# One joint routing job for the first batch's keys and first queries, a second job for its other queries, and query blocks of varying width

## The chip, the cores and the metric

The kernel runs on one core of one Trainium2 chip. The metric is the device time of one execution in microseconds (us), lower is better. Executions carry a state, fast or slow, and only fast ones enter the ratios. All profiles shown are of executions in the fast state.

Engines are named as in the profile: PE is TensorE, PEld its weight loads, DVE is VectorE, ACT is ScalarE, POOL is GpSimd, SP is SyncE. Names such as L102 are lines of the kernel in question, so they differ between kernels.

## The reference

Attention in which a query sees only the keys with the same nearest centroid, then an expert layer over all tokens:

```python
batch, n_heads, seq, head_dim, n_clusters = 4, 8, 768, 64, 16
q_assign = argmax(q_n @ c_n)            # nearest of 16 centroids, for each head
k_assign = argmax(k_n @ c_n)
mask     = q_assign[:, :, :, None] == k_assign[:, :, None, :]
scores   = where(mask, q @ k.T / sqrt(64), -1e9)
x        = softmax(scores) @ v          # then heads side by side: 3072 tokens x 512
h        = x @ w_in                     # 512 -> 2048
out      = (h * sigmoid(h)) @ w_out     # 2048 -> 512
```

## The kernel before

Heads are handled in pairs; a batch has four pairs, and the first batch is the one that nothing can hide. For each pair the fp32 queries and keys are loaded (`nat`), split into a high and a low fp16 half (`hl`), transposed (`abt`; by PE in the first batch, by a transposing DMA later), multiplied with the split centroids (`psL`), and routed. Routing is a list of VectorE instructions: transpose the products (`lt`), take the maximum over each 16 (`mx`), compare (`oht`), transpose back (`ohu`). The resulting one-hot rows are copied below the queries and keys, so that one matmul (`st`) gives score plus mask. Then come the exponential (`P`, ACT), the product with the values (`pv`, PE), the division (`xh`, VectorE), a transposition (`xt`), and the expert layer: `ph` with `win_s`, tanh (`tn`, ACT), the gate (`gt`, VectorE), `po` with `wout_s`, and the store.

The first batch is routed pair by pair, and a block is always 256 queries wide:

```python
def load(p, t):                                      # one load per pair, queries or keys
    nat = mp.tile([128, 2, NJ * D], f32, name=f"nat{t}", bufs=3)
    nc.sync.dma_start(nat, (q, k)[t][b, 2 * r : 2 * r + 2]. ...)

def split_hi(p, t, eng):
    hl = hls[p, t] = mp.tile([128, 2 * NJ, 2, D], f16, name="hl", bufs=5)
    ...
groups = {}
for pl in [[p] for p in range(HB)] + [[p, p + 1] for p in range(HB, NP, 2)]:   # first batch: single pairs
    groups[pl[-1]] = pl
```

The centroids are split into halves on POOL, ahead of POOL's own loads (values `vt`, then the weights `win_s` and `wout_s`):

```python
def centroid_split():
    cn = mp.tile([128, D], f32, name="cn")
    nc.gpsimd.tensor_scalar(out=cn, in0=craw, scalar1=cw, scalar2=OHV, op0=ALU.mult, op1=ALU.mult)
    for n in range(2):
        nc.gpsimd.tensor_copy(ch2[:, n, :], cn)
    for n in range(2):
        nc.gpsimd.tensor_tensor(out=cl2[:, n, :], in0=cn, in1=ch2[:, n, :], op=ALU.subtract)
```

One property of the program matters for all that follows. A list scheduler inside the kernel simulates the engines while the kernel is being built, and writes each engine's instructions in the order that its own estimates give. On the chip this order is fixed: an engine whose next instruction waits does nothing, even if a later one could run (the changed kernel's VectorE stands 7.43 us in this way, see below).

The softmax here doesn't subtract the row's maximum and nothing guards it: scores larger than these inputs give would overflow.

## Time and profile before

| | before |
|---|---|
| time, median of 3 | 322.22 us (321.57 to 322.32) |
| span of the profiled execution | 322.0 us |
| first routing (VectorE `lt`) | 14.56 us |
| first exponential (ACT `P`) | 19.64 us |
| first expert matmul (PE `ph`) | 47.68 us |
| useful PE work of the whole program | 290 us |
| PE time lost by 60 us | 28.9 us |

"PE time lost by X" is X less the useful PE work begun by X, each matmul counted at the duration that it has where matmuls stand back to back (for 128 columns, which only the changed kernels have in `st` and `ph`, 56 ns, see below). It is read from the trace, and it is the yardstick for everything below, because between 60 us and the tail this kernel loses nothing. In all kernels below the account falls by 2 to 4 us between 60 and 300 us unless said otherwise, because those unit durations are slightly high.

The lines that carry the reading of the bound are in the prediction. One more view is needed, because the result turned on it. These are POOL's first instructions in the timeline of the kernel before (columns: start us, busy us, engine, line, operation, out<-in, shape, count, and in brackets the idle time before and what ended it):

```profile
5.16 0.31 POOL L346 TENSOR_SCALAR cn<-craw,cw 128x64 f32<-128x64 f32 x1 [3.54 <-DVE cw L342]
...
7.88 6.95 POOL L89 DMA_DIRECT2D vt<-in_v_dram  x8
```

POOL waits 3.54 us for the centroids' norm, splits them, and only then, at 7.88 us, issues the value loads. The reader should see that this small job is also a lock on the value loads, which nobody wrote down as one.

### The profile page before, as it was taken

The page shows a single profiled execution, that of the slowest core. Times are in us where ns is not written, and L with a number is a line of the kernel's source. Part 1 is how long each engine was busy: PE and PEld are TensorE (multiplying, and loading weights), DVE is VectorE, ACT ScalarE, POOL GpSimd, SP SyncE. Part 2 cuts the span into 40 slices and gives each one's busy share as a digit, 9 for nine tenths or more (in the row PEclk, how much of TensorE's full clock was granted, in tenths as well). Part 3 has the DMA queues.
Part 4 walks back from the last instruction along what each step waited for, and adds up shares of the span by engine and source line. Part 5 has one row for each costly group of instructions (what it writes and reads, how often), then busy time and mean ns, then how long its engine had stood idle before and what let it go on. Part 6 is the DMA issues. An engine that isn't in the chain of part 4 may idle for free.

```text
span 322.0 us, 7812 instructions
## 1 busy us (share of the span) xinstructions
PE 302.5 (94%) x3316; PEld 225.5 (70%) x3316; DVE 190.2 (59%) x356; ACT 239.3 (74%) x279; POOL 35.3 (11%) x57
## 2 busy tenths in 40 slices
PE   6688795999999999999989999999999999999994
PEld 4565574876877768777677777777777787786651
DVE  5798983675856878438328877338444344254431
ACT  5896994985678979886878787886787787786420
POOL 4952100024000000023200000040000000000000
PEclk9799998999999999999999999999999999999999
DMA  7999999999926990394996970293310200200001
GB/s 213 289 240 239 235 186 149 214 149 132 223 67 183 210 231 9 77 129 61 191 243 155 223 147 11 75 166 25 69 41 17 66 35 28 74 0 35 33 35 65
DMA packets 89843, 40.00 MB, mean 124 GB/s; under 512 B 75216, under 2 KB 86224, under 8 KB 89808
## 3 DMA queue, kind: packets, MB, share of 16 engines
q1 hardware_dynamic: 62032, 32.16, 44.1%
q0 software_dynamic: 27776, 7.34, 22.8%
q8 instruction: 26, 0.43, 0.6%
q14 instruction: 9, 0.07, 0.1%
HBM read 27.30 MB, written 6.29 MB: 104 GB/s over the span
## 4 chain that ended last, share of the span: by engine, by line
PE 78%; DMA 9%; DVE 9%; ACT 1%; issue 1%; SPq 1%; DVEq 0%
PE ph L276 25%; PE po L298 24%; PE st L213 16%; PE pv L229 9%; DMA abt<-hl 6%; PE psL L155 3%; DMA nat<-in_q_dram 2%; DMA xt<-xh 2%; DVE hl L102 1%; DVE abt L205 1%; DVE ohu L187 1%; DVE lt L162 1%; DVE hl L97 1%; DVE mx L173 1%; DVE oht L180 1%
## 5 line engine op out<-in xcount | busy, mean ns | idle before, releaser
L219 ACT ACTIVATE P<-st,bias 128x1024 f16<-128x1024 f32 x144 | 156.7, 1114 | 36.6 <-PE st L213 36.1
L285 DVE SCALAR_TENSOR_TENSOR gt<-tn,ph 128x512 f16<-128x512 f32 x96 | 65.1, 683 | 61.1 <-ACT tn L282 60.4
L276 PE MATMUL ph<-xt,win_s 128*128 128x256 f16 x768 | 97.1, 274 | 4.1 <-DVE xh L243 3.3
L298 PE MATMUL po<-wout_s,gt 128*128 128x512 f16 x384 | 96.5, 379 | 1.1 <-DVE ot L307 1.1
L213 PE MATMUL st<-abt 80*128 80x256 f16 x576 | 85.5, 274 | 4.0 <-ACT abt L203 1.6
L276 PEld LDWEIGHTS <-win_s 128*128 128x128 f16 x768 | 74.1, 98 | 18.1 <-DVE xh L243 3.6
L282 ACT ACTIVATE tn<-ph,zbias 128x512 f32<-128x512 f32 x96 | 65.3, 686 | 25.3 <-PE ph L276 24.7
L213 PEld LDWEIGHTS <-abt 80*128 80x128 f16 x576 | 55.1, 98 | 26.5 <-issue 3.7
L298 PEld LDWEIGHTS <-gt 128*128 128x128 f16 x384 | 35.9, 97 | 29.1 <-issue 1.6
L89 POOL DMA_DIRECT2D vt<-in_v_dram x32 | 26.5, 833 | 174.0 <-PE pv L229 165.2
L229 PE MATMUL pv<-vt,P 128*128 128x65 f16 x1152 | 43.3, 193 | 0.2 <-ACT P L219 0.2
L229 PEld LDWEIGHTS <-P 128*128 128x128 f16 x1152 | 41.8, 98 | 2.1 <-ACT P L219 0.3
L102 DVE SCALAR_TENSOR_TENSOR hl<-nat,hl 128x768 f16<-128x768 f32 x32 | 29.8, 956 | 2.8 <-ACT hl L95 2.5
L307 DVE TENSOR_SCALAR ot<-po 128x512 f32<-128x512 f32 x24 | 16.5, 686 | 24.2 <-PE po L298 24.1
L242 DVE RECIPROCAL rz<-pv 128x4 f32<-128x4 f32 x48 | 8.6, 178 | 28.0 <-PE pv L229 27.6
L243 DVE TENSOR_TENSOR xh<-pv,rz 128x256 f16<-128x256 f32 x48 | 20.4, 424 | 1.7
L97 DVE TENSOR_SCALAR hl<-nat 128x768 f16<-128x768 f32 x19 | 10.4, 556 | 5.3 <-DMA abt<-hl 5.2
L268 PE MATMUL warm<-idle,ident 128*128 128x256 f16 x66 | 11.7, 316 | 1.7 <-POOL ident masks.py:199 1.7
L95 ACT ACTIVATE hl<-nat 128x768 f16<-128x768 f32 x13 | 11.0, 843 | 2.6 <-DMA nat<-in_q_dram 2.2
L155 PE MATMUL psL<-abt,wh 128*32 128x512 f16 (+1 forms) x128 | 10.5, 340 | 0.7 <-DVE abt L122 0.4
L187 DVE STREAM_TRANSPOSE ohu<-oht 128x768 f16<-128x768 f16 x10 | 9.8, 977 | 0.9 <-DVE oht L180 0.5
L117 PE MATMUL ptt<-ident,hl 128*128 128x128 f16 x96 | 7.7, 235 | 2.7 <-ACT abt L122 1.9
(52 smaller groups left out, 100.4 us busy)
## 6 DMA issues: line engine op xcount, KB each, us to landing
nat<-in_q_dram SPq DMA_DIRECT2D x16, 384.0 KB, 5.2
nat<-in_k_dram SPq DMA_DIRECT2D x16, 384.0 KB, 5.6
out_dram<-ot SPq DMA_DIRECT2D x24, 256.0 KB, 2.1
vt<-in_v_dram POOLq DMA_DIRECT2D x32, 96.0 KB, 5.1
win_s<-in_moe_w_in_dram POOLq DMA_DIRECT2D x4, 512.0 KB, 13.2
wout_s<-in_moe_w_out_dram POOLq DMA_DIRECT2D x4, 512.0 KB, 22.9
abt<-oh SPq DMA_DIRECT2D x48, 24.0 KB, 2.0
abt<-hl SPq DMA_TRANSPOSE x24, 4.5
```

The source lines that it names most:

```text
L89: nc.gpsimd.dma_start(vts[p % NV][:, h, :, 0:D], v[b, 2 * r + h].rearrange("(p j) d -> p j d", j=NJ))
L102: nc.vector.scalar_tensor_tensor(out=hl[:, :, 1, :], in0=nat, scalar=128.0, in1=hl[:, :, 0, :], op0=ALU.mult, op1=ALU.subtract)
L155: nc.tensor.matmul(psL[g : g + 32, 0 : hi - lo], w, x[:, lo:hi], start=first, stop=last)
L213: nc.tensor.matmul(st[:, a, h, :], ab[0:K, 1, h, ts(2 * s + a, 128)], ab[0:K, 0, h, ts(u, UQ)], start=True, stop=True)
L219: nc.scalar.activation(out=P, in_=sts.pop((n, s)), func=AF.Exp, bias=bias32, scale=ESC)
L229: nc.tensor.matmul(out[:, e, h, :], P[:, a, h, ts(e, 128)], vts[p % NV][:, h, 2 * s + a, 0 : D + 1], start=(s + a + h + e == 0), stop=(s = ...
L243: nc.vector.tensor_tensor(out=xhs[c][:, :, r], in0=out[:, :, :, 0:D], in1=rz.unsqueeze(3).to_broadcast([128, 2, 2, D]), op=ALU.mult)
L276: nc.tensor.matmul(ph[:, e].rearrange("p (g x) -> p g x", g=2), win_s[:, r, ts(2 * f + e, 128)], xts[c][:, :, r, :], start=(r == 0), stop= ...
L282: nc.scalar.activation(out=tn, in_=phs[c, f], func=AF.Tanh, bias=zbias, scale=0.5)
L285: nc.vector.scalar_tensor_tensor(out=gts[c][:, 2 * f : 2 * f + 2, :], in0=tns.pop((c, f)), scalar=1.0, in1=phs.pop((c, f)), op0=ALU.add, o ...
L298: nc.tensor.matmul(pos[c, s], gts[c][:, fc, ts(s, 128)], wout_s[:, fc, :], start=(fc == 0), stop=(fc == NFB - 1))
L307: eng.tensor_scalar(out=ot, in0=pos.pop((c, s)), scalar1=0.5, scalar2=None, op0=ALU.mult)
```

## The change

The intent is to start the expert layer earlier. The keys of all four pairs and their first 256 queries (1024 columns) are routed in one job instead of four; the other 512 queries follow in a second job. The first batch's query blocks are 128, 128, 256 and 256 wide, so the first expert block needs less attention work ahead of it. For this the query loads are cut into a part "A" (first 256 queries) and a wide part "B" (the other 512). Besides, the centroid split moves from POOL to ACT and VectorE, there are eight split buffers instead of five, nine for exponentials instead of twelve, and the scheduler gets new estimates, a `HOLD` for POOL's loads and a table of hand-made rank shifts (`PLAN`).

```diff
+    SPAN = {"K": (0, NJ), "A": (0, 2), "B": (2, NJ)}
...
-    def load(p, t):
+    def load(p, t, v, eng):
-        nat = mp.tile([128, 2, NJ * D], f32, name=f"nat{t}", bufs=3)
+        nat = mp.tile([128, 2 * NJ * D], f32, name=f"nat{t}", bufs=4)[:, 0 : 2 * (hi - lo) * D]
...
+        hl = hls[p, t, v] = mp.tile([128, 2 * NJ, 2, D], f16, name="hl", bufs=8)[:, 0:n]
...
+    def logits0(v):
+        if v == "K":
+            both = ps.tile([128, 2, 512], f32, name="psL2", tag="st", bufs=2)
+            outs = [(both[:, 0], 1, 0, 512), (both[:, 1, 0:256], 1, 512, 768), (both[:, 1, 256:512], 0, 0, 256)]
+        else:
+            psL = ps.tile([128, 512], f32, name="psL", tag="moe", bufs=3)
+            outs, tl = [(psL, 0, 256, 768)], [psL]
...
-    def centroid_split():
-        cn = mp.tile([128, D], f32, name="cn")
-        nc.gpsimd.tensor_scalar(out=cn, in0=craw, scalar1=cw, scalar2=OHV, op0=ALU.mult, op1=ALU.mult)
+    def centroid_high():
         for n in range(2):
-            nc.gpsimd.tensor_copy(ch2[:, n, :], cn)
+            nc.scalar.mul(ch2[:, n, :], craw, cw)
+    def centroid_low():
         for n in range(2):
-            nc.gpsimd.tensor_tensor(out=cl2[:, n, :], in0=cn, in1=ch2[:, n, :], op=ALU.subtract)
+            nc.vector.scalar_tensor_tensor(out=cl2[:, n, :], in0=craw, scalar=cw, in1=ch2[:, n, :], ...)
...
+    HOLD = 7.8
+    W0 = (1, 1, 2, 2)
+    RK = {'K': -395, 'A': -400, 'B': -270}
...
+    def held(t):
+        return t > HOLD - 1e-6
...
+            {"POOL": 1.8}, lambda e: load_v(p), ..., when=from_slot(begins[p] - LEAD_V) if b else held, dma=(1.25, 2.0, 1.0),
+            wins = [Piece({"POOL": 0.6}, lambda e, r=r: e.dma_start(win_s[:, r], win_v[:, r]), (), rank=-6, when=held, ...)]
...
+    PLAN = {12: (40, 0), 15: (-4, 0), ...}
```

The cuts are marked with dots; the functions that use these names change accordingly.

## The prediction

> **What bounds the kernel now.** I read the page first (busy shares, the 40 slices), then the stretches, then the chain of waits, then the timeline of the first 60 us. The page:
>
> ```profile
> PE 302.5 (94%) x3316; PEld 225.5 (70%) x3316; DVE 190.2 (59%) x356; ACT 239.3 (74%) x279; POOL 35.3 (11%) x57
> ...
> PE   6688795999999999999989999999999999999994
> ```
>
> PE is full from the eighth slice on. So what can still be won lies in the first 60 us and in the tail. The stretches say the same (columns: length, then busy us and count of PE, PEld, DVE, ACT, POOL; clock, DMA share, GB/s):
>
> ```profile
> 10.00:15.00 5.00, 3.90 (x47) 2.80 (x47) 4.92 (x8) 4.47 (x10) 4.83 (x6) 0.76 1.68 271
> 15.00:20.00 5.00, 3.85 (x38) 3.11 (x36) 4.77 (x10) 4.38 (x7) 3.50 (x6) 0.89 1.85 236
> 20.00:25.00 5.00, 4.85 (x69) 3.63 (x69) 4.88 (x9) 5.00 (x7) 1.65 (x3) 1.00 1.08 232
> ...
> 80.00:120.00 40.00, 40.00 (x440) 29.78 (x438) 28.77 (x49) 31.11 (x38) 1.07 (x2) 1.00 0.90 181
> ```
>
> From 10 to 25 us VectorE (third pair) is busy 14.6 of 15 us: it bounds the start. PE's own digits there flatter it, for they hold warming matmuls and modelled ends. So I priced PE's useful work from pieces of the chain that stand back to back: 8 ph 0.872 us, 4 po 0.864, 8 st 0.875, 32 psL 1.41 (16 in the first batch 0.76), 24 pv 0.87 and 18 transposes 1.17 (timeline). 768 ph = 83.7, 384 po = 82.9, 576 st = 63.0, 1152 pv = 41.8, psL 6 x 1.41 + 4 x 0.76 = 11.5, 112 transposes = 7.3: 290 us of a span of 322. By 60 us the trace has started 96 transposes, 64 psL, 100 st, 168 pv, 32 ph, 4 po: 31.3 us of work, so 28.7 us are lost there. The tail after PE's last matmul takes 4.0. Together that covers the 32, within 1 us: between 60 and 318 us nothing is lost.
>
> Why the start is slow, in the chain of waits and in the timeline:
>
> ```profile
> 9.76 0.96 DVE hl L102
> 11.71 1.26 PE ptt L117 x18
> 12.96 1.58 PE psL L155 x16
> 16.82 0.99 DVE ohu L187
> 19.09 1.83 DVE hl L102 x2
> 21.43 0.96 DVE hl L102
> 25.09 0.99 DVE ohu L187
> 30.98 0.98 DVE ohu L187
> 35.59 0.99 DVE ohu L187
> ...
> 41.03 11.09 DMA abt<-hl
> 53.31 1.64 PE ph L276 x8
> ```
>
> ```profile
> 34.29 12.18 ACT L219 ACTIVATE P<-st,bias 128x1024 f16<-128x1024 f32 x12 [0.59 <-PE st L213]
> ...
> 52.14 0.56 DVE L97 TENSOR_SCALAR hl<-nat 128x768 f16<-128x768 f32 x1 [5.25 <-DMA abt<-hl]
> ...
> 53.31 1.64 PE L276 MATMUL ph<-xt,win_s 128*128 128x256 f16 x8 [3.28 <-DVE xh L243]
> ```
>
> Four routings, one per pair, end at 16.8, 25.1, 31.0 and 35.6 us. Until the fourth is through, ACT has done 6 exponentials; then it does 12 in a row. The expert layer's first block needs all four pairs, so its matmuls begin at 47.7, and stop again at 50: VectorE stands 5.25 us before a split for the second batch whose output buffer a transposing DMA still reads.
>
> **What the Trainium skill says.** "VectorE: DVE Perf Modes", section on the TRN2 errata: a VectorE instruction that reads SBUF pays a fixed extra per instruction, so a few large ones beat many small. The trace agrees: tensor_reduce over 384 elements takes 0.552 us; at 0.96 GHz (that page) the elements are 0.40, so 0.15 is fixed. "TensorE: Matmul & The Clock Gate", section "Back-to-back issue gap": a stream of weight load and matmul at 128 columns has about 81 ns per matmul, more per column than a wide one. The trace has 65 ns (18 transposes in 1.17 us) against 109 ns for 256 columns; I use 65. "DMA: Bandwidth & Descriptors", section "Queues, rings and completion order": each engine goes round its queues packet by packet. The trace agrees: packets of 1536 B of the hardware queue start at 246 per us between 8 and 11 us, when it is alone, at some 100 beside the value loads, and at 40 to 50 between 25 and 30 us, one for one with the 4096 B packets of win_s. "GPSIMD Engine Reference", section "Instruction dispatch": the first call to a freshly loaded library pays about 6 us that no instruction shows. No trace here shows that yet.
>
> **The change, part by part.**
> Removed on VectorE: four routings of 1.12 + 0.55 + 0.56 + 0.98 = 3.2 us, 12.8 in all. Added: keys and first 256 queries (1024 columns): transposes 2 x 0.71, reduce and compare 0.15 + 1024/960 = 1.22 each, back-transpose 0.98 x 4/3 = 1.30: 5.2 us. The other 512 queries: 0.71 + 0.68 + 0.68 + 0.65 = 2.7. Saved: 4.9. The one-hot copies go from 16 to 24 smaller ones (about 7 us instead of 5.8, split with ACT), and splits in parts repeat the fixed 0.15. Net about 3 us of VectorE.
>
> More important is the order. The first expert block is now 128 queries wide and needs one joint routing and 8 exponentials instead of four routings and 12. The order of the changed kernel puts on VectorE ahead of that routing: 1 high key split 0.56, 4 low ones 3.84, centroid 0.44, splits of the first queries 3 x 0.29 + 4 x 0.42 = 2.6, of the other queries 3 x 0.43 + 4 x 0.69 = 4.1, 2 copies 1.1: 12.6 us. The first low split began at 5.58 before and can do so again. Keys and first queries are 2.1 MB; before, 2.46 MB had moved by 10 us, so the last part lands at about 11 and the first query part at about 10, and VectorE waits some 2.4 us. Routing starts at 5.6 + 12.6 + 2.4 = 20.6, ends at 25.8, three copies 0.8, first st and exponential at 27 (before 19.6, but then starved). An exponential of 768 columns I put at 0.87 (1.114 for 1024; copies of 768 take 0.80 to 0.84). Eight: 34.0. Then pv, normalise, transpose, copy, 2 us: the first ph at 36 instead of 47.7 and, after the gap, 53.3.
>
> PE's useful work by 36: transposes 6.2, psL 2.8, 13 groups of 6 st at 65 ns 5.1, 5 half pv 2.2, xp 0.3: 16.6. Lost: 19.4. After that PE isn't full at once, since a block of half width feeds it for 7 us while the next needs exponentials; I allow 3 us. The 5.25 us wait of VectorE goes: eight split buffers instead of five let all eight splits of batch two go without a DMA having to finish. New cost on PE: 192 st of 128 columns for 96 of 256, 12.5 against 10.5, and 128 ph for 64, 8.3 against 7.0: 3.3 us. Sum: 290 + 3.3 + 19.4 + 3 + 4.0, less the 1 us by which this account exceeds the span before = 318.7. The rest is neutral: from 60 us on PE has no gaps, and the last order of ph and po (eight pairs, then 32 po) is the same.
>
> **The rivals.**
> 1. The gap is not 3 us but nearly none, and first queries come sooner: 315. For it: ACT in the first 80 us has less work than PE. Against it: VectorE's in-order list ahead of the routing.
> 2. The other 512 queries come late. Their four loads can only start once VectorE has split the first ones, near 11 to 13 us, and in the trace before the value packets run from 11.1 to 19.9 and win_s from 19.4 to 33.6. At 100 packets per us, then 45, their 1024 packets need about 10 us: landing near 24 or 25. The order puts their splits ahead of the joint routing on VectorE, so routing then starts at about 26 and everything moves by 5 us: 323 to 324. I hold this for nearly as likely as the plan.
> 3. The value loads start early. Before, POOL split the centroids until 7.9 us and only then issued them; now nothing stands ahead of them but memsets, at 2 us, and first packets would flow at 5.4 (3.25 us after the issue, as before). Then key and query loads share the engines from the start, most query packets meet win_s at 45 per us, and the first routing slips to near 38: 330 or more. Against it: the schedule in the source holds these loads to 7.8 us, as if a trace had shown POOL not free before, which the library load would explain.
> 4. A new bound in the steady stretch (shorter distance between score groups, 9 instead of 12 buffers for exponentials): PE has been full there, so this could only cost; I give it 1 us at most.
>
> **Range and chances.** The plan gives 318.7, rival 2 323.5, rival 1 315, rival 3 over 330. Weights of about 0.45, 0.28, 0.15, 0.12. I predict 318.5 us, 313 to 327 eight times in ten. Faster by over 2% means under 315.8: 0.2. Slower by over 2% means over 328.7: 0.13. Within: 0.67.
>
> **What would show it.** Right: one transposing group of 1024 columns at 20 to 26 us, the first exponential at about 27, first ph near 36, no 5 us wait of VectorE for abt<-hl, PE full from about 45 us, the tail unchanged. Rival 2: VectorE's split of the wide query part waits for nat<-in_q_dram for 3 to 6 us around 18 to 25. Rival 3: the first vt issue at 2 us. The prediction is wrong if PE shows gaps after 60 us, or if the first ph comes before 32 or after 45.

## The result, and the profile after

| | before | changed |
|---|---|---|
| time, median | 321.93 us (4 runs, 321.57 to 322.32) | 330.38 us (4 runs, 329.29 to 334.14) |
| ratio changed / before | | 1.0283, 95% interval 1.0201 to 1.0365: slower |
| span of the profiled execution, granted clock | 322.0 us, 0.989 | 328.7 us, 0.969 |
| useful PE work | 290 us | 290.3 us |
| PE time lost by 60 us | 28.9 us | 36.9 us |

A ratio here is the mean time of one kernel's fast runs over that of the other's fast runs of the same rounds, so it is not quite the ratio of the medians quoted beside it. The change is slower by 2.8%, outside the predicted range.

The page of the changed kernel: busy shares, then PE, VectorE and the granted PE clock in 40 slices of 8.2 us.

```profile
PE 301.8 (92%) x3422; PEld 228.4 (69%) x3422; DVE 193.5 (59%) x381; ACT 234.0 (71%) x278; POOL 38.5 (12%) x60
...
PE   7714778999999999999999999999999999999994
...
DVE  6604894799583488957348886634343354455441
...
PEclk9775997999999999999999999999999999999999
```

The loss is in one place. PE's third slice holds a 1, and VectorE's third a 0; from the eighth slice on PE is as full as before. The stretches show it finer (same columns as in the prediction):

```profile
10.00:15.00 5.00, 3.86 (x39) 3.22 (x40) 4.76 (x9) 3.98 (x7) 3.10 (x5) 0.80 2.14 188
15.00:20.00 5.00, 2.29 (x25) 1.98 (x22) 0.00 (x0) 2.59 (x4) 1.48 (x2) 0.84 1.07 229
20.00:25.00 5.00, 0.00 (x0) 0.00 (x0) 0.43 (x1) 0.00 (x0) 0.00 (x0) 0.50 1.07 230
25.00:30.00 5.00, 0.90 (x8) 0.77 (x8) 2.04 (x5) 0.00 (x0) 0.38 (x1) 0.50 1.14 223
```

VectorE, which the prediction took for the limit of this stage, runs at full load up to 15 us and then for 2.47 of 15 us. From 20 to 25 us neither PE nor ACT does anything, the granted PE clock is down to 0.50, and only the DMA goes on, at 223 to 230 GB/s. VectorE's timeline names what it waits for:

```profile
14.30 0.55 DVE L130 COPY abt<-ptt 128x768 f16<-128x768 f16 x1
22.28 0.43 DVE L102 TENSOR_SCALAR hl<-nat 128x512 f16<-128x512 f32 x1 [7.43 <-DMA nat<-in_q_dram]
27.89 0.43 DVE L102 TENSOR_SCALAR hl<-nat 128x512 f16<-128x512 f32 x1 [5.18 <-DMA nat<-in_q_dram]
...
33.68 1.31 DVE L180 STREAM_TRANSPOSE lt<-psL 128x512 f32<-128x512 f32 x2 [1.91 <-PE psL L170]
```

A split of 512 columns is one of the wide part B. Two of these splits wait 7.43 and 5.18 us for their loads. The joint routing, of keys and part A, starts at 33.68 us, although its own loads had long been there: the key and A packets had all moved by 10.4 us. It is simply behind B's splits in VectorE's order (and so is a last copy of transposed keys, at 28.96 us, without which its products on PE cannot begin). The chain of waits says the same (start us, duration us, what):

```profile
11.28 16.59 DMA nat<-in_q_dram
...
33.68 1.33 DVE lt L180 x2
...
51.83 1.71 PE ph L305 x16
...
56.05 1.79 PE ph L305 x32
...
87.33 1.75 PE ph L305 x16
```

One load, issued at 11.28 us, takes 16.59 us to land. (The last two lines also give a price: 32 matmuls of 128 columns take 1.79 us, 56 ns each, and 16 of 256 columns 1.75 us, 109 ns each.) The reason why the load is so slow is in POOL's timeline:

```profile
1.58 6.92 POOL L93 DMA_DIRECT2D vt<-in_v_dram  x8
9.27 0.56 POOL L598 DMA_DIRECT2D win_s<-in_moe_w_in_dram  x1 [0.76 <-DMA vt<-in_v_dram]
```

The value loads are issued at 1.58 us, not at 7.88: with the centroid split gone from POOL, nothing holds them. `HOLD = 7.8` is only a figure in the scheduler's simulation; on the chip no wait stands for it. So POOL issues 6.3 us earlier, and its packets start some 5 us earlier. In the trace's records of packets the 128-byte value packets now start at 5.9 us (before: 11.1), and the 4096-byte packets of `win_s` at 14.6 (before: 19.4). The wide query loads are issued between 9.08 and 11.80 us, because they wait for buffers that the splits of part A must free; their first packet starts at 13.1 us. Between 16 and 26 us their 1024-byte packets move at 42 to 53 per us beside 43 to 45 per us of `win_s`, and the last starts at 29.5.

### The profile page after: what moved, and what is told of

Its sections match the earlier page's. It is cut to its first block, busy times and chain, and to the rows that moved or that the text cites. A ratio compares the mean times of both kernels' runs of the same rounds, so it can differ in the third digit from the quotient of the medians.

```text
span 328.7 us, 8037 instructions
## 1 busy us (share of the span) xinstructions
PE 301.8 (92%) x3422; PEld 228.4 (69%) x3422; DVE 193.5 (59%) x381; ACT 234.0 (71%) x278; POOL 38.5 (12%) x60
## 4 chain that ended last, share of the span: by engine, by line
PE 83%; DMA 7%; DVE 6%; ACT 1%; SPq 1%; issue 1%; ACTq 0%; DVEq 0%
PE ph L305 26%; PE po L329 25%; PE st L232 18%; PE pv L252 10%; DMA nat<-in_q_dram 7%; PE psL L153 3%; DVE abt L217 2%; PE psL L170 1%; SPq L87 1%; ACT P L240 1%; DVE ot L338 1%; DVE lt L180 1%; DVE oht L190 1%; DVE ohu L197 1%; DVE mx L184 1%
## 5 line engine op out<-in xcount | busy, mean ns | idle before, releaser
L240 ACT ACTIVATE P<-st,bias 128x1024 f16<-128x1024 f32 (+1 forms) x148 | 157.7, 1093 | 21.9 <-PE st L232 20.7
L305 PE MATMUL ph<-xt,win_s 128*128 128x256 f16 (+1 forms) x832 | 99.6, 266 | 0.0
L232 PE MATMUL st<-abt 80*128 80x256 f16 (+2 forms) x624 | 86.9, 265 | 3.1 <-ACT P L240 1.9
L305 PEld LDWEIGHTS <-win_s 128*128 128x128 f16 x832 | 75.8, 99 | 13.3
L232 PEld LDWEIGHTS <-abt 80*128 80x128 f16 (+1 forms) x624 | 56.9, 98 | 24.6 <-issue 4.1
L106 DVE SCALAR_TENSOR_TENSOR hl<-nat,hl 128x768 f16<-128x768 f32 (+2 forms) x36 | 30.2, 864 | 0.3
L266 DVE RECIPROCAL rz<-pv 128x4 f32<-128x4 f32 (+1 forms) x52 | 9.2, 178 | 25.4 <-PE pv L252 24.8
L102 DVE TENSOR_SCALAR hl<-nat 128x768 f16<-128x768 f32 (+2 forms) x28 | 13.9, 513 | 14.8 <-DMA nat<-in_q_dram 14.1
L122 PE MATMUL ptt<-ident,hl 128*128 128x128 f16 x96 | 8.9, 256 | 14.7 <-DVE hl L106 14.6
L267 DVE TENSOR_TENSOR xh<-pv,rz 128x256 f16<-128x256 f32 (+1 forms) x52 | 21.0, 404 | 1.8
L122 PEld LDWEIGHTS <-hl 128*128 128x128 f16 x96 | 7.3, 115 | 16.5 <-DVE hl L106 15.9
L100 ACT ACTIVATE hl<-nat 128x768 f16<-128x768 f32 (+2 forms) x8 | 6.1, 762 | 13.5 <-DMA nat<-in_q_dram 13.1
L180 DVE STREAM_TRANSPOSE lt<-psL 128x512 f32<-128x512 f32 (+1 forms) x15 | 8.3, 587 | 2.4 <-PE psL L170 1.9
## 6 DMA issues: line engine op xcount, KB each, us to landing
wout_s<-in_moe_w_out_dram POOLq DMA_DIRECT2D x4, 512.0 KB, 20.6
```

Source lines behind the costliest of these rows:

```text
L106: nc.vector.scalar_tensor_tensor(out=hl[:, :, 1, :], in0=nats[p, t, v], scalar=128.0, in1=hl[:, :, 0, :], op0=ALU.mult, op1=ALU.subtract)
L122: nc.tensor.transpose(pt[:, j, :], hl[:, i * NJ + j].rearrange("p c d -> p (c d)"), ident)
L232: nc.tensor.matmul(cols(st, n)[:, a, h, :], ab[0:K, 1, h, ts(A * s + a, 128)], ab[0:K, 0, h, 128 * j0 : 128 * (j0 + w)], start=True, stop= ...
L240: nc.scalar.activation(out=P, in_=st, func=AF.Exp, bias=bias32, scale=ESC)
L267: nc.vector.tensor_tensor(out=xhs[c][:, 0:w, p % HB], in0=out[:, 0:w, :, 0:D], in1=rz[:, 0:w].unsqueeze(3).to_broadcast([128, w, 2, D]), o ...
L305: nc.tensor.matmul(ph.rearrange("p (e g x) -> p e g x", e=n, g=w)[:, e], win_s[:, r, ts(n * f + e, 128)], xts[c][:, 0:w, r, :], start=(r = ...
```

## The experiments

The theory after this reading (call it the starved load): B's packets reach the DMA engines together with the weights and get about half the turns, and VectorE's fixed order turns the lateness of B into lateness of everything. Its rivals: that VectorE's order alone is at fault whatever the loads do; that the change's plan was too optimistic even with the loads in time, so that no repair would reach 318.7; that the wait of 5.25 us was worth nothing; and that the narrow blocks cost more than they win. All kernels gave correct results.

| experiment | time, median (fast runs) | ratio to before, 95% interval | routing starts | first exponential | first `ph` | lost by 60 us |
|---|---|---|---|---|---|---|
| changed kernel | 330.38 (4) | 1.0283 (1.0201 to 1.0365) | 33.68 | 40.70 | 51.65 | 36.9 |
| weights after B | 319.45 (19 of 20) | 0.9958 (0.9937 to 0.9979) | 21.14 | 28.14 | 37.85 | 23.6 |
| values after the keys | 316.05 (4) | 0.9868 (0.9818 to 0.9918) | 19.14 | 26.15 | 35.97 | 22.6 |
| own buffer for A | 315.63 (3 of 4) | 0.9823 (0.9778 to 0.9867) | 20.60 | 27.61 | 37.44 | 22.2 |
| routing ahead of B's splits | 318.25 (12) | 0.9933 (0.9908 to 0.9958) | 19.85 | 26.90 | 41.25 | 25.9 |
| before, 8 split buffers | 323.47 (8) | 1.0069 (1.0035 to 1.0103) | | | 49.91 | 27.6 |
| both load repairs | 318.07 (4) | 0.9879 (0.9837 to 0.9921) | 18.09 | 25.11 | 34.75 | 22.7 |
| both, B told to land late | 320.55 (20) | 0.9961 (0.9940 to 0.9982) | 17.81 | 25.25 | 36.17 | 27.7 |
| centroid split back on POOL | 321.55 (20) | 0.9996 (0.9980 to 1.0011) | 18.71 | 25.68 | 36.05 | 23.5 |
| own buffer, second block turned on PE | 321.66 (20) | 1.0015 (0.9995 to 1.0035) | 20.23 | 27.24 | 36.87 | 23.1 |
| both repairs, second block turned on PE | 320.24 (16) | 0.9968 (0.9940 to 0.9996) | 18.19 | 25.20 | 34.97 | 22.3 |
| values after the keys, 256-wide blocks, no shifts | 334.69 (4) | 1.0387 (1.0330 to 1.0445) | 19.06 | 27.43 | 44.17 | 28.3 |
| values after the keys, no shifts | 319.84 (19 of 20) | 0.9947 (0.9923 to 0.9971) | 18.98 | 27.35 | 36.18 | 26.5 |

The kernel before, run beside them, had medians of 320.79 to 321.59 us. The experiments ran in three groups of four, each on a chip of its own (the first four, the next four, the last four); between groups the ratios are the better comparison. Medians are of all runs; where a run fell in the slow state, the number of fast ones is given.

### Weights after B

Only POOL's queue changes: ahead of the first load of `win_s` it writes one element of that buffer from the last B buffer, so it waits for B. All other engines run the same instructions in the same order.

```diff
-  lambda e, r=r: e.dma_start(win_s[:, r], win_v[:, r])
+  lambda e, r=r: (r or e.tensor_copy(win_s[:, 0, 0:1], nats[HB - 1, 0, "B"][:, 0, 0:1]),
+                  e.dma_start(win_s[:, r], win_v[:, r]))
```

> The changed kernel with one POOL copy of a single column put ahead of the first load of win_s; the copy reads the last part of the queries, so no weight packet can flow before all queries have landed. Every other instruction stands in the same order. Theory A (the wide query part is starved by the packets of win_s, and VectorE's list stands on it ahead of the joint routing): the last query part lands near 17 to 18 us instead of 28, the joint routing's first transpose starts near 21.5 instead of 33.7, the first exponential near 28.5 instead of 40.7, and the time falls to 318 (316 to 321). Theory B (the start is long by itself: longer joint routing, 128-wide matmuls, cold clock): the routing moves by less than 4 us and the time stays above 326.

It took 319.45 us. The values still leave at 1.6 us; only the weights wait. POOL stands from 8.2 us until the last B load has landed at 18.1; then, from POOL's and VectorE's timelines:

```profile
18.83 2.17 POOL L598 DMA_DIRECT2D win_s<-in_moe_w_in_dram  x4 [0.30 <-POOL win_s L598]
```

```profile
16.59 0.43 DVE L102 TENSOR_SCALAR hl<-nat 128x512 f16<-128x512 f32 x1 [1.31 <-DMA nat<-in_q_dram]
...
21.14 1.30 DVE L180 STREAM_TRANSPOSE lt<-psL 128x512 f32<-128x512 f32 x2
```

The waits of 7.43 and 5.18 us shrink to 1.31 at most, routing starts 12.5 us earlier, and B's packets run from 13.3 to 17.5 us. So 13.3 us of PE's lost time (36.9 to 23.6) were due to the weights' packets beside B's. Holding the weights is not free, though: another 1.8 us are lost between 60 and 80 us (23.6 to 25.4), where the changed kernel and the next two, with the same order, lose 0.4 at most. At 64.17 us PE waits 1.07 us there for a transposing DMA of the second batch (`abt<-hl`); why that one comes late was not traced.

### Values after the keys

The same device one step earlier: the first value load waits for the last key load. This puts back, by a true dependence, about the time at which the kernel before issued the values.

```diff
-  lambda e: load_v(p)
+  lambda e: (p or e.tensor_copy(vts[0][:, 0, 0, 0:1], nats[HB - 1, 1, "K"][:, 0, 0:1]), load_v(p))
```

> The changed kernel with a POOL copy ahead of the first value load that waits for the last key load: POOL issues its first load near 7.5 us, as in the kernel before (7.9), instead of 1.6. Same order otherwise. If the early issue is the cause (my third rival): first value packets near 11 us, win_s from 19, the wide query part meets value packets alone, lands near 19 to 21, time 319 to 322. If the query part is late with values on their way too (my second rival alone): landing near 24 to 25, routing near 27 to 30, time 323 to 327. If neither matters: 330.

It took 316.05 us, better than the 319 to 322 expected if the early issue was the cause. From POOL's and VectorE's timelines:

```profile
8.29 6.62 POOL L93 DMA_DIRECT2D vt<-in_v_dram  x8 [0.31 <-POOL vt L587]
```

```profile
14.49 0.65 DVE L102 TENSOR_SCALAR hl<-nat 128x512 f16<-128x512 f32 x1 [0.63 <-DMA nat<-in_q_dram]
...
19.14 1.30 DVE L180 STREAM_TRANSPOSE lt<-psL 128x512 f32<-128x512 f32 x2
```

B's packets run from 10.2 to 16.4 us, over before the first packet of `win_s` at 18.9. The longest wait of VectorE for B is 0.63 us. One dependence on POOL, with the same order on every other engine, takes the kernel from 2.8% slower to 1.3% faster.

### An own buffer for part A

The opposite remedy: POOL's early issue stays, and what is removed is the reason why B's loads are issued late. Part A gets a buffer of its own (it borrows one of `gt`, not needed until later), so B's loads wait for nobody.

```diff
-  nat = mp.tile([128, 2 * NJ * D], f32, name=f"nat{t}", bufs=4)[:, 0 : 2 * (hi - lo) * D]
+  nat = (qa()[:, 256 * p : 256 * p + 256] if v == "A"
+         else mp.tile([128, 2 * NJ * D], f32, name=f"nat{t}", bufs=4))[:, 0 : 2 * (hi - lo) * D]
+  # qa(): one tile [128, 1024] f32 with tag "gt"
```

> The changed kernel with the first query parts in a buffer of their own (borrowed from one that is used later), so that the four wide query loads wait for no buffer and are issued from about 4 to 6 us on instead of 9.1 to 11.8. Same order on all engines. Theory A: they run beside the value packets only and land by 15 to 17 us, routing near 20, first exponential near 27, time 317 to 320. Theory B: above 326.

It took 315.63 us, the lowest median of the study and below the 317 to 320 expected. SP's timeline of the changed kernel and then of this one shows the eight query loads:

```profile
2.27 9.94 SPq L87 DMA_DIRECT2D nat<-in_q_dram  x8
```

```profile
2.27 2.33 SPq L87 DMA_DIRECT2D qa<-in_q_dram  x4
4.64 3.42 SPq L87 DMA_DIRECT2D nat<-in_q_dram  x4
```

And what VectorE and ACT make of it:

```profile
20.60 1.31 DVE L181 STREAM_TRANSPOSE lt<-psL 128x512 f32<-128x512 f32 x2 [0.75 <-PE psL L171]
```

```profile
27.61 8.81 ACT L241 ACTIVATE P<-st,bias 128x768 f16<-128x768 f32 x11
```

The last B load is issued at 7.69 us instead of 11.80, B's packets run from 9.8 to 15.3 us, and the first packet of `win_s` starts at 17.2. Here the values' packets do share the engines with B's, and it does no harm. So the early values are harmful only through what comes behind them: they bring `win_s` forward into B. The order of instructions is again that of the changed kernel on every engine. Its interval overlaps that of the run before, so which of the two remedies is better isn't settled.

### Routing ahead of B's splits

Here the loads stay as bad as they are, and the scheduler is told the truth about them: B lands some 12 us later than its estimate had it. It then puts the joint routing ahead of B's splits on VectorE; PE's and ACT's lists change with it.

```diff
-  dma=(1.03 * size, 1.7, 1.5),
+  dma=(1.03 * size, 14.0 if v == "B" else 1.7, 1.5),
```

> The changed kernel with the loads left as they are, but the scheduler is told that the wide query part lands 12 us later, so that VectorE's list has the joint routing ahead of its splits. Theory A's second half (the in-order list makes the lateness cost): the wide part still lands at 22 to 28 us, but the routing starts at 18 to 20 us, the first exponential at 25 to 28, time 317 to 321. If the lateness of the wide part itself is what costs, because the later blocks need it: above 325.

It took 318.25 us. B's packets still run until 29.4 us, yet from VectorE's and ACT's timelines:

```profile
19.85 1.31 DVE L180 STREAM_TRANSPOSE lt<-psL 128x512 f32<-128x512 f32 x2 [2.01 <-PE psL L170]
```

```profile
26.90 1.69 ACT L240 ACTIVATE P<-st,bias 128x768 f16<-128x768 f32 x2
...
31.40 0.90 ACT L240 ACTIVATE P<-st,bias 128x768 f16<-128x768 f32 x1 [0.61 <-PE st L232]
```

The late load alone doesn't delay the routing; the fixed order is the other half of the cause. Each half can be taken away by itself, and the large loss goes. But what comes behind the routing now meets B: ACT has gaps between the first exponentials, B's splits come back among the divisions, and `ph` begins at 41.25 instead of 36 to 37.5. By the medians, loads in time are worth 2 to 3 us more than the order; of the two load repairs only the own buffer has an interval clear of this one.

### The kernel before with eight split buffers

The prediction counted on the 5.25 us wait of VectorE for a split buffer to go. This experiment takes that one part of the change alone, on the kernel before.

```diff
-  hl = hls[p, t] = mp.tile([128, 2 * NJ, 2, D], f16, name="hl", bufs=5)
+  hl = hls[p, t] = mp.tile([128, 2 * NJ, 2, D], f16, name="hl", bufs=8)
```

> The kernel before, with eight split buffers instead of five: one part of the change alone. In the trace before, VectorE stood 5.25 us for a buffer that a transposing DMA was reading and PE lost about 4 us of work in that stretch. If that wait is a good part of what the whole change can win: 318 (316 to 320), and no VectorE wait of over 3 us for abt<-hl. If the wait only moves elsewhere: 320 to 322.

The wait is gone, and the kernel took 323.47 us, 0.7% slower. VectorE's longest wait from 36 to 62 us is now 1.77 us, but the first `ph` starts at 49.91 us instead of 47.68, and PE's lost time by 60 us falls by only 1.3 us and is back at 29.0 by 80 us. The scheduler was told of the buffers too and moved other instructions, so this isn't the wait by itself, and what the wait alone is worth stays open. With the list that comes with eight buffers, nothing is gained.

### Both load repairs

> Both remedies at once: first value load behind the last key load, and the wide query loads free of the buffer wait. With the value loads held back VectorE had no wait over 1 us between 4 and 37 us, so if its list of splits is now what sets the routing's start, the routing starts within 0.7 us of 19.1 and the time is that of the value hold alone: 315 to 316.5. If loads still bound the start: routing at 17 or earlier, 313 to 314.5.

Values after the keys and the own buffer for A together gave 318.07 us. That is a miss against both expectations (315 to 316.5, or 313 to 314.5), and by the ratios no better than either repair alone. B's packets run from 8.1 to 11.8 us, and the first `ph` starts at 34.75 us, 1 to 3 us earlier than with one repair. By 50 us 19.7 us are lost, by 60 us 22.7. PE's timeline has the place:

```profile
51.82 1.89 PE L306 MATMUL ph<-xt,win_s 128*128 128x128 f16 x16 [1.49 <-DMA xt<-xh]
```

PE waits there for the transposing DMA of the second narrow block; the order was made for a later start. That takes back the lead of the earlier start. It does not account for the further 1.6 us between the profiled executions (317.48 against 315.87), which the lost time shows only after 120 us.

### Both repairs, and B told to land late

The scheduler got a B latency of 7.0 us instead of 1.7 on top of the two repairs.

> Both remedies, and the scheduler told that the wide part lands 5.3 us later, so that its list has the joint routing ahead of three of the four low splits of the wide part. VectorE's list then holds about 10 us of work ahead of the routing instead of 12.6: routing near 16 to 17, first exponential near 23.5, first ph near 34 to 35, time 313 to 315. If the displaced splits only come back between the exponentials (as with the wide part late: first ph at 41 in spite of a first exponential at 27): 316 to 318.

A miss: 320.55 us. Routing (17.81 us) and the first `ph` (36.17) are early, but PE waits 3.19 us for the same transposing DMA at 52.48 us, and lost time rises from 22.5 us at 50 to 27.7 at 60.

### Centroid split back on POOL

This undoes one part of the change alone: POOL splits the centroids as before and is thereby kept from the value loads.

```diff
-        nc.vector.tensor_scalar(out=cw, in0=cw, scalar1=OHV, scalar2=None, op0=ALU.mult)
-    def centroid_high(): ...                 # ACT
-    def centroid_low(): ...                  # VectorE
+    def centroid_split(): ...                # POOL, as in the kernel before
```

> The changed kernel with only the centroid part of the diff undone: POOL normalises and splits the centroids again, and so cannot issue value loads before about 7.5 us. If this part of the diff is what made the change lose: 315 to 318, first value packets near 10 to 11 us, routing near 19 to 21. If not: 326 or more.

The start came as expected: values issued at 8.97 us, B's packets from 11.2 to 16.4, routing at 18.71, first `ph` at 36.05, 23.5 us lost by 60. This ties the early values to the moved centroid split. The total missed: 321.55 us. Removing instructions from ACT and VectorE gave the scheduler another list, and this list loses 4.7 us between 60 and 80 us (23.5 to 28.2), where VectorE waits for ACT's tanh:

```profile
64.72 1.28 DVE L316 SCALAR_TENSOR_TENSOR gt<-tn,ph 128x512 f16<-128x512 f32 x2 [5.55 <-ACT tn L312]
```

The expectation of 315 to 318 took the rest of the list as unchanged, and it wasn't.

### The second block turned on PE

If the transposing DMA of the second narrow block is what PE waits for, PE could turn that block itself. This was tried with the own buffer alone and with both repairs.

```diff
-    XPE = (0, 2)
+    XPE = (0, 1, 2)
```

> First query parts in their own buffer, and besides the second block's attention output (128 queries) is turned on TensorE instead of by a transposing DMA. If the pause of PE between 50 and 60 us is the latency of that DMA, the lost time by 60 us falls from 20.6 to about 19.5 and the time from 315.6 to about 314.5. If PE has other work in that pause, nothing changes (315 to 316).

> Both remedies for the loads (values held behind the keys, first query parts in their own buffer) and the second block turned on TensorE. With the transposing DMA, PE waited 1.5 us for it at 51.8 us and gave back what the earlier start had won (318.1). If that wait was what gave it back: lost time by 60 us falls from 21.2 to about 19, and the time to 314 to 315.5. If the earlier start is given back in any case, because exponentials bound this stretch: 317 to 318.5.

Both missed: 321.66 and 320.24 us. (The table, at 56 ns for 128 columns, has 22.2 and 22.7 us of lost time for the 20.6 and 21.2 that these expectations start from.) The waits of `ph` for the DMA are gone, but from 55.6 to 61.5 us (with both repairs, two us earlier) PE now waits time and again for exponentials (0.18 to 0.55 us ahead of each `st` group), then VectorE waits 3.7 us for a tanh, and lost time rises to 27.2 and 26.0 us by 120 us. From 50 to 120 us these two kernels lose 6 to 7 us; the same kernels without the turn lose nothing there and 2 us. By the ratios, turning that block on PE, with the list that follows from it, costs about 6 us with the own buffer and 3 us with both repairs. The edit adds an instruction to the list, and the shifts by hand were renumbered to name the same ones; that they fit one list only is a likely reason, but not a shown one.

### The blocks' width

To learn what the narrow blocks are worth, the first batch was cut into three blocks of 256, with the joint routing kept and values after the keys. The shifts by hand name positions of the old list and had to be off, so a second kernel with 128, 128, 256, 256 and the shifts off is the one to compare with.

```diff
-    W0 = (1, 1, 2, 2)
+    W0 = (2, 2, 2)            # with an order of units and a last block to match
-    for i, (shift, which) in PLAN.items():
+    for i, (shift, which) in ():
```

> Values held behind the keys, and the first batch in three blocks of 256 queries as before instead of 128, 128, 256, 256; joint routing and second job kept. The hand-made rank shifts of the change don't fit the new list and are off, so it is to be compared with the next run, which has them off too. The plan gave the narrow first block 8 exponentials of 0.87 us ahead of the first ph instead of 12 of 1.1, so wide blocks begin ph about 5 us later (near 41 us) but lose none of the 128-column cost, which was measured as nearly nothing: if the narrow block is worth what the plan said, 2 to 4 us slower than the next run; if PE's backlog of score groups fills the wait anyway, the same within 1 us.

> Values held behind the keys, blocks of 128, 128, 256, 256 as in the change, hand-made rank shifts off: the control of the run before. The shifts reach the start as well as the steady stretch; if they are worth little, 316 to 318 as with them on (316.1); if they matter, 319 to 322, with PE time lost between 40 and 100 us.

With wide blocks 334.69 us, with narrow ones 319.84: 14.9 us, far more than the 2 to 4 expected. The first `ph` comes at 44.17 instead of 36.18 us: 8 us, not 5. But by 60 us the difference in lost time is only 1.8 us (28.3 against 26.5), and by 120 us it is 13.3 (40.3 against 27.0). So most of the 14.9 us is a list for wide blocks that nobody tuned, and only the 8 us at the first `ph` speaks for the width itself. The shifts by hand are worth 2.5 us by the ratios (0.9947 against 0.9868; 3.8 by the medians, which are from different chips), lost between 50 and 60 us.

## Why the prediction was wrong

**The bound and the plan's arithmetic held.** PE is full from about 60 us, and what is won or lost lies ahead of it. With the loads in time the plan's milestones come out:

| | plan | values after keys | own buffer | changed kernel |
|---|---|---|---|---|
| joint routing starts | 20.6 | 19.14 | 20.60 | 33.68 |
| first exponential | 27 | 26.15 | 27.61 | 40.70 |
| first `ph` | 36 | 35.97 | 37.44 | 51.65 |
| lost by 60 us | 22.4 | 22.6 | 22.2 | 36.9 |
| time | 318.7 | 316.05 | 315.63 | 330.38 |

The 22.4 is the plan's 19.4 plus its allowance of 3. The joint routing takes 5.1 us from 33.68 to 38.8 us, as against the 5.2 worked out from the fixed part of a VectorE instruction.

**One term of the plan was wrong: the 3.3 us for 128-column matmuls.** The count was wrong: 96 `st` of 128 columns stand for 48 of 256 in the trace, not 192 for 96. The price was wrong too: 56 ns, not 65, which came from PE's transposes. The term is 224 x 0.056 - 112 x 0.109 = 0.3 us. With it the plan gives 315.7, and the two repaired kernels took 316.05 and 315.63. An agreement this close is partly luck: the kernel before had 320.79 beside them, not the plan's 322.

**The step that failed is the reading of when POOL's loads go.** The prediction had both halves of the cause. Rival 2 had the wide query part late and its splits ahead of the routing; rival 3 had the values issued at 2 us. So the plan's sum has 2.4 us of waiting on VectorE ahead of the joint routing, for the keys and first queries, and nothing for B, whose splits it counts in the same list; the trace has 12.6 us of waits for B alone (7.43 and 5.18). Rivals 2 and 3 do have B late, but the prediction treated them as alternatives, and gave rival 3 a weight of 0.12 because the source "holds these loads to 7.8 us, as if a trace had shown POOL not free before, which the library load would explain". The trace has the first issue at 1.58 us, no library load, and the hold is a figure in the scheduler alone. Reading `held` would have settled it: it is a condition on the scheduler's simulated time and leaves no instruction behind.

**The two are one mechanism, and neither costs much alone.** Rival 2 was computed with `win_s` starting at 19.4 us, as before, so that part of B would get through beside the values. With the values at 1.58 us `win_s` starts at 14.6, 1.5 us after B's first packet, and B has it as company for 12.6 of its 16.4 us. Hence 29.5 us for the last packet instead of 24 to 25, and routing at 33.7 instead of 26. Rival 2's 5 us became 13.1 (33.68 against the plan's 20.6); some 1.6 of these are the products of the joint routing, which took 3.5 us on PE at a granted clock of 0.50 instead of 1.9 in "values after the keys". By itself rival 2 did not come about: with the values held, B's loads were still issued at 8.9 to 10.8 us, but their 1024 packets took 6.2 us (166 per us, not 100 and then 45), and VectorE waited 0.63 us. And the early values without a late B cost nothing, as the own buffer shows.

**Rival 3 had the right number and half of the path.** It said 330 or more, and 330.38 came. It said that most query packets meet `win_s`, at 45 per us: part B, which is half of the 2048 query packets, met it for most of its way, at 42 to 53. But it also slowed the key and first query loads, and that hardly happened: beside the values, part A's packets moved at 278 per us from 8 to 10 us and were through by 10.4, against 8.8 with the values held. And it lacked the buffer wait that makes B late: with the own buffer the values leave at 1.59 us and no such loss is seen. So the harm comes through `win_s` alone, and that rival 3's number fits so well is partly luck.

**The 5.25 us wait goes, and what it was worth was not isolated.** In the changed kernel the wait for `abt<-hl` is gone, as predicted. But in the kernel before, more split buffers alone gave nothing (1.0069). The plan's time did not add the 5.25 us as a term, so its sum isn't hurt. The trace of the kernel before does tie PE's gap to this wait: `ph` waits 3.28 us for a division that stands right behind the waiting split on VectorE and begins at 52.83 us. But with the gap closed and the list re-made, the time didn't fall, so the gap's length is no measure of what closing it wins.

**Rival 4** was right in that the steady stretch gains nothing. As long as the list of the change is kept, it loses nothing either.

**Two readings were loose, without effect on the sum.** The 16.8, 25.1, 31.0 and 35.6 us at which the four routings "end" are the starts of their last step, which takes 1 us. And the counts named for the 31.3 us of useful work by 60 us give 30.7; ten further transposes, not named, make up the rest.

**What stays open.** Why B's first packet starts 4.0 us after its first issue is not shown: the value packets flow at 1150 per us from 10 to 12 us, and with the values held it was 1.3 us, but the records don't say what the queue did in between. Nor is it shown in full why re-made lists lose 4 to 7 us between 50 and 120 us; only that five do (both repairs with a late B, the POOL split, the two with the second block turned on PE, and the one without shifts). The list with routing ahead of B's splits loses nothing past 50 us. A part of it stands in the traces: in all five the granted PE clock is at 0.50 for 3.4 or 6.8 us, from about the end of PE's pause on. These are the stretches of both repairs with the second block turned on PE, and then of the own buffer alone (columns as before; the third from the end is the clock):

```profile
60.00:65.00 5.00, 4.93 (x55) 3.09 (x57) 2.01 (x5) 3.90 (x5) 0.00 (x0) 0.50 1.22 217
```

```profile
60.00:65.00 5.00, 5.00 (x79) 3.19 (x77) 4.90 (x10) 3.60 (x5) 0.00 (x0) 1.00 0.65 123
```

PE is as busy in both, but in the first 24 `pv` take 1.52 us, and 0.90 us later at full clock. Half of 3.4 or 6.8 us is 1.7 or 3.4 us of PE work, an estimate of what such a stretch costs on top of the pause. "Both load repairs" has one too, from 51.7 us, and so has the kernel before, from 53.6; "values after the keys" and the own buffer have none between 40 and 300 us. The first of these two is without one although PE stands idle for 1.9 us between 50 and 55 us, so which pauses bring it, and what starts the pauses in the re-made lists, stays open.

## What to carry to other kernels

Removing work from an engine also removes whatever that work was holding back: list what the engine issues next, and ask which queue it will now reach early and whom it meets there. A time in a scheduler's model is not a wait on the chip; if a load must not go before another, make it depend on it, and one such dependence was worth 4% here (1.0283 to 0.9868). In a fixed instruction order, an instruction whose load is uncertain should not stand ahead of the one that everybody waits for, and two pessimistic cases that share a resource must be computed together, not weighed as alternatives.

## What the Trainium skill lacked or had wrong

- "TensorE: Matmul & The Clock Gate", section "Back-to-back issue gap", gives about 81 ns per matmul for a stream with weight loads at 128 columns. Here 32 `ph` of 128 columns, each with its weight load, took 1.79 us, 56 ns each. The figure that the page keeps for the isolated gap (section "Wait — 56ns, not 53.3ns?", 55.6 ns warm) is the one that held in this stream.
- "GPSIMD Engine Reference", section "Instruction dispatch", has about 6 us for the first call to a freshly loaded library. It doesn't say that POOL can issue DMAs without paying it: here the first load was issued at 1.58 us, right after the memsets.
- "DMA: Bandwidth & Descriptors", section "Queues, rings and completion order", has the engine go round the queues packet by packet. The trace agrees in kind: 42 to 53 packets of 1024 B per us beside 43 to 45 of 4096 B. The page lacks the consequence in bytes: one side moved 43 to 54 KB per us and the other 176 to 184, so here the load with the small packets got about a fifth of the bytes. It also says nothing of how long a load can take to its first packet beside many small packets of another queue: here 4.0 us beside 1150 value packets per us, 1.3 us with the values held (the cause of the difference is not shown).
- The same page, section "Latency and other measured facts", gives about 1 us to the first byte for loads issued by GpSimd. Here the first packet of the values, which are cast from fp32 to fp16 as they load, started 4.3 us after POOL began to issue (1.58 to 5.9 us), and 3.2 us after it in the kernel before (7.88 to 11.1).
